# RWKV-7 attention with a SoLU block on one core: two products turned over, one head's features as weights

## The chip, the core and the metric

The kernel runs on one core of one Trainium2 chip. The metric is the device time of one execution in microseconds (us); three executions of the kernel before took 1791.39, 1779.59 and 1787.28, median 1787.28. All arithmetic is float32. TensorE (PE) executes one float32 product as two instruction pairs, each a weight load (PEld in the profile) and a stream of the other operand, so counts in the trace are twice the counts of products in the program.

## The reference: what is computed

Four batches, eight heads, 768 tokens, 40 features a head. Each head keeps a 40 x 40 state that every token reads, decays and updates; the outputs of the eight heads are laid side by side (320 features) and go through a dense layer of 1024, a softmax-weighted activation, a normalisation and a dense layer back to 320.

```python
for t in range(S):
    y[:, :, t] = np.einsum('bhd,bhde->bhe', rt, state)
    Sa = np.einsum('bhde,bhe->bhd', state, at)
    state_decay = state * wt[:, :, None, :] - np.einsum('bhd,bhe->bhde', Sa, bt)
    state = state_decay + np.einsum('bhd,bhe->bhde', vt, kt)
...
x = np.ascontiguousarray(attn_out.transpose(0, 2, 1, 3)).reshape(B * S, H * D)
h = x @ w_in
e = np.exp(h - h_max)
sm = e / (np.sum(e, axis=-1, keepdims=True) + 1e-09)
solu = h * sm
ln = (solu - mu) / np.sqrt(var + 1e-06) * g_ln
return (ln @ w_out).astype(np.float32)
```

## The kernel before

The tokens are cut into 24 chunks of 128 tokens of one batch. Within a chunk the recurrence is a triangular system (I + N) U = X0, one 128 x 128 system per head, so a chunk is a chain of matrix products. The main loop takes chunk i through its second half while chunk i + 1 goes through its first half; `in_turn` emits the pieces of two parts by turns, a `yield` ending a piece.

- `decay` takes the logs of the decays and, by products with 0/1 matrices, sums them along the chunk: `pcum`. Line 247 gives the factors of the keys, line 250 (320 columns) those of `a` and of the output, and line 252 (four products with 4 columns each) the factors that carry the state to mid-chunk and to the end.
- `attend` transposes `a`, `b`, `k`, `v` and `r` (`transposed`, line 199, copied out by ScalarE at line 201) and forms 128 x 128 score matrices per head (`scores`, line 209, masked by VectorE at line 211): `nt` (the matrix N), `psi`, `lamv`. Their products contract over 64 rows; the even heads lie in rows 0 to 63 and the odd heads in rows 64 to 127.
- `solve` inverts I + N of the next chunk by doubling: five levels of `py` (line 315), `pz` (line 325) and a transposition `pt` (line 299), each with two halves p that VectorE and ScalarE serve in between, and one last level (lines 340 and 347). It is most of TensorE's work and is what the other parts are interleaved with.
- `recurrence`: `px` (lines 363 and 366) gives X0 (tile `x0`); `pu` (line 373) multiplies it by the inverse: the 128 x 128 inverse of a head is the weights and 40 columns of X0 stream. ScalarE negates it into `nu` (128 tokens x features). The state update `pst` (line 381) uses `nu`; `nu` is transposed into `nuT` for the scores `lamu`.
- `finish` is `readout` and `mlp`. In `readout`, `pyo` collects r times the state (line 408) and, for each head, `lamv` and `lamu` as 128 x 128 weights with 40 columns of the keys streaming (line 413). VectorE scales the result (line 417, tile `x`), three transpositions `pxT` (line 421) and a ScalarE copy (line 423) make `xT`, the weights of `h` (line 433). `mlp` then runs the activation on VectorE and ScalarE, transposes the result (`plnT`, line 465) and multiplies by the second matrix (`po`, line 470).

The order of instructions on each engine is set by a scheduler at build time that emits what its own model finds ready by priority; at run time each engine follows that order and waits on semaphores. Loads and stores are issued by the SP queue in its order.

Of the kernel before, what the change touches and what calls it, by code (L numbers as in the profile page):

```python
# [56 lines left out]
def kernel(  # L57
# [25 lines left out]
    NK = -(-DM // P)  # L83
# [34 lines left out]
    lw_t = zeroed("lw", [P, H, 64], 2)  # L118
    ah_t = zeroed("ah", [P, H, 64], 2)
# [5 lines left out]
    x_t = zeroed("x", [P, NK * P], 2)  # L125
    y_lev = zeroed("ylev", [P, 2, G, P], len(LEVELS))
    y_last = const.tile([P, 2, G, 64], FP32, name="y_last")
    w_in = zeroed("w_in", [P, NK, DFF], 1)[0]
# [44 lines left out]
    def weights():  # L173
        nc.scalar.dma_start(out=g_rows, in_=moe_g_ln.rearrange("(c p) -> c p", p=P))
        for kt in range(NK):
            n = min(P, DM - kt * P)
            load_weight(w_in[0:n, kt, :], moe_w_in[kt * P:kt * P + n, :])
# [17 lines left out]
    def transposed(name, src, tag="T", bufs=4):  # L195
        """[128 tokens, 8 x 64] -> [(head of the pair, feature), pair, 128 tokens]"""
# [4 lines left out]
        nc.scalar.copy(out=o.rearrange("p g t -> p (g t)"), in_=t)  # L201
        return o

    def scores(name, lhs, rhs, dst):
        """dst[s, head, t] = lhs_s . rhs_t where s < t, else 0"""
# [18 lines left out]
    def load(i):  # L224
# [7 lines left out]
        for n, ap in (("w", w), ("k", k), ("b", b), ("a", a)):  # L232
            d["raw_" + n] = raw.tile([P, H, D], FP32, tag="raw_" + n, name="raw_" + n)
            nc.sync.dma_start(out=d["raw_" + n], in_=src(ap))
        nc.sync.dma_start(out=rv[:, 1, :, 0:D], in_=src(v))
        nc.sync.dma_start(out=rv[:, 0, :, 0:D], in_=src(r))

    def decay(i):
        """The decayed keys of chunk i, their growth and decay counted from mid-chunk."""
        d = st[i]  # L240
        lw, kb, ah = lw_t[i % 2], kb_t[i % 3], ah_t[i % 2]
        d["kb"] = kb
        nc.scalar.activation(out=lw[:, :, 0:D], in_=d["raw_w"], func=AF.Ln)
        ex = d["ex"] = two.tile([P, DM + 16], FP32, tag="ex", name="ex", bufs=4)
# [4 lines left out]
        t = bank("pcum")  # L249
        nc.tensor.matmul(t[:, 0:DM], lhsT=c_("cum_ex"), rhs=lw[:, :, 0:D], start=True, stop=True)  # L250
        for g in range(G):
            nc.tensor.matmul(t[:, DM + 4 * g:DM + 4 * g + 4], lhsT=pair(lw, g), rhs=c_("half"),
                             start=True, stop=True)
        nc.scalar.activation(out=ex, in_=t[:, 0:DM + 16], func=AF.Exp)
        for j, n in enumerate("kb"):
            nc.gpsimd.tensor_tensor(out=kb[:, j, :, 0:D], in0=d["raw_" + n], in1=heads(inv), op=ALU.mult)
        nc.gpsimd.tensor_tensor(out=ah[:, :, 0:D], in0=d["raw_a"], in1=heads(ex[:, 0:DM]), op=ALU.mult)
        f = ex[:, DM:].rearrange("p (g f c) -> p g f c", g=G, f=2)
# [4 lines left out]
        d["ah"] = ah  # L263

    def attend(i):
        """What chunk i needs of itself alone: its tokens' products with each other."""
        d = st[i]
        kb = d["kb"]
        aT = d["aT"] = transposed("aT", d["ah"], "aT", 2)
# [65 lines left out]
        # the last doubling is one block of 64 x 64, and T itself is not needed any more  # L335
# [17 lines left out]
    def recurrence(i):  # L353
# [14 lines left out]
        x0 = two.tile([P, DM], FP32, tag="x0", name="x0")  # L368
        nc.scalar.copy(out=x0, in_=t[:, 0:DM])
        yield  # L370
        t = bank("pu")
        for h in range(H):
            nc.tensor.matmul(t[:, h * D:h * D + D], lhsT=d["tinvT"][:, h % 2, h // 2, :],  # L373
                             rhs=x0[:, h * D:h * D + D], start=True, stop=True)
        nc.scalar.mul(out=nu[:, :, 0:D], in_=heads(t[:, 0:DM]), mul=-1.0)
# [16 lines left out]
        nuT = transposed("nuT", nu)  # L392
        lamu = d["lamu"] = wide("lamu", 1)
        scores("lamu", nuT, d["rT"], lamu)
# [6 lines left out]
    def readout(i):  # L401
# [4 lines left out]
        if ci:  # L406
            for g in range(G):
                nc.tensor.matmul(t[:, g * 80:g * 80 + 80], lhsT=d["rT"][:, g, :],
                                 rhs=d["sT"][:, g, :].rearrange("p (c d) -> p c d", c=2)[:, :, 0:D],
                                 start=g == 0, stop=False, skip_group_check=True)  # L410
        for h in range(H):
            for j, lam in enumerate((d["lamv"], d["lamu"])):
                nc.tensor.matmul(t[:, h * D:h * D + D], lhsT=lam[:, h % 2, h // 2, :], rhs=kb[:, j, h, 0:D],  # L413
                                 start=not ci and h == 0 and j == 0, stop=j == 1, skip_group_check=True)
        yield
        x = x_t[i % 2]
        nc.vector.tensor_tensor(out=x[:, 0:DM], in0=t[:, 0:DM], in1=d["ex"][:, 0:DM], op=ALU.mult)
# [25 lines left out]
        # (q / c - mean) / sqrt(var / c^2 + eps) = (q - mean_q) / sqrt(var_q + eps c^2), c = esum + 1e-9  # L443
# [86 lines left out]
```

## Time and profile before

| | |
|---|---|
| three executions | 1791.39, 1779.59, 1787.28 us (median 1787.28) |
| profiled execution, span of its instructions | 1769.0 us |
| PE busy, PEld busy | 91%, 80% of the span |
| DVE, ACT, POOL busy | 32%, 23%, 14% |
| mean granted TensorE clock | 0.898 of full speed |
| chain that ended last: PE, DVE, issue, ACT | 80%, 10%, 5%, 4% |

The profile gives the span, from the first to the last instruction; the lowest of the three executions is 10.6 us and the median 18.3 us above it. PE is the matrix stream, PEld the weight load that runs beside it, DVE is VectorE, ACT is ScalarE, POOL is GpSimd and SP issues transfers. A line Lnn is the line of the kernel printed above. The granted clock has two levels, 2.4 GHz (1.0) and 1.2 GHz (0.5); a stretch that shows 0.72 was partly at each.

### The profile page before, as it was taken

Reading aid. Unit: us, or ns where it says so; the run is one execution under the profiler, and the core shown is the slowest. Engines: PE = TensorE matmul, PEld = TensorE weight load, DVE = VectorE, ACT = ScalarE, POOL = GpSimd, SP = SyncE. Lnnn points to the kernel's source line nnn. Section 1 sums busy time; section 2 is a strip of 40 time slices with the busy share of each in tenths; the row PEclk is TensorE's granted clock in tenths of the full one; section 3 lists DMA queues with packets and bytes.
Section 4 is the critical chain, followed back from the end, with each engine's and each line's share of the span. In section 5 each row is a group of like instructions: output and inputs, shape, how many; then the busy total and the mean of one; then the engine's idle time right before and its main releaser. Section 6 shows DMA issues by size and latency. Waiting matters only on the chain.

```text
span 1769.0 us, 26279 instructions
## 1 busy us (share of the span) xinstructions
PE 1607.7 (91%) x11353; PEld 1407.5 (80%) x11353; DVE 570.5 (32%) x1306; ACT 399.5 (23%) x765; POOL 242.6 (14%) x274
## 2 busy tenths in 40 slices
PE   3999999899999999999989989999999999998997
PEld 2888787787877878879778778788787887877875
DVE  7783222322232222222232332223222322222231
ACT  1122122221221222222222222122122222222221
POOL 6131010210110101101021021011010110102100
PEclk9689898998998988988999999899898998898996
DMA  7220110100101101011011010010110100000000
GB/s 133 54 60 8 20 27 4 23 12 19 24 5 23 27 5 23 12 20 23 5 23 27 4 23 16 16 23 5 23 27 4 19 12 16 5 4 1 5 4 4
DMA packets 157267, 34.95 MB, mean 20 GB/s; under 512 B 150616, under 2 KB 154720, under 8 KB 157152
## 3 DMA queue, kind: packets, MB, share of 16 engines
q1 hardware_dynamic: 153216, 27.54, 8.6%
q10 hardware_dynamic: 3936, 5.75, 1.1%
q8 instruction: 89, 1.46, 0.3%
q14 instruction: 26, 0.21, 0.0%
HBM read 29.34 MB, written 3.93 MB: 19 GB/s over the span
## 4 chain that ended last, share of the span: by engine, by line
PE 80%; DVE 10%; issue 5%; ACT 4%; DMA 1%; POOL 1%; POOLq 0%; ACTq 0%
PE py L315 15%; PE pz L325 13%; PE po L470 7%; PE h L433 7%; PE pt L299 6%; PE pyo L413 5%; PE pu L373 2%; PE plamv L209 2%; PE px L366 2%; PE plamu L209 2%; DVE tinvT L328 2%; PE pst L381 2%; PE plnT L465 2%; PE ppsi L209 2%; PE pnt L209 2%
## 5 line engine op out<-in xcount | busy, mean ns | idle before, releaser
L315 PEld LDWEIGHTS py<-tinv,nt 128*128 128x128 f32 x1920 | 283.6, 233 | 24.0 <-ACT tinv L300 13.0
L315 PE MATMUL py<-tinv,nt 128*128 128x64 f32 x1920 | 292.4, 317 | 0.7 <-ACT tinv L300 0.5
L325 PE MATMUL pz<-tinvT,ylev 128*128 128x64 f32 x1920 | 271.1, 301 | 0.9 <-DVE ylev L317 0.9
L325 PEld LDWEIGHTS pz<-tinvT,ylev 128*128 128x128 f32 x1920 | 262.8, 218 | 5.9 <-DVE ylev L317 1.0
L300 ACT COPY tinv<-pt 128x512 f32<-128x512 f32 x288 | 165.8, 587 | 328.8 <-PE pt L299 302.6
L299 PE MATMUL pt<-cst,tinvT 128*128 128x128 f32 x1152 | 189.4, 300 | 21.7 <-DVE tinvT L328 16.8
L317 DVE TENSOR_TENSOR ylev<-py,cst 128x256 f32<-128x256 f32 x240 | 101.6, 423 | 258.6 <-PE py L315 258.6
L299 PEld LDWEIGHTS pt<-cst,tinvT 128*128 128x128 f32 x1152 | 147.6, 160 | 45.1 <-DVE tinvT L328 44.0
L328 DVE TENSOR_TENSOR tinvT<-tinvT,pz 128x256 f32<-128x256 f32 x240 | 100.7, 419 | 255.3 <-PE pz L325 255.2
L303 POOL TENSOR_TENSOR tinvT<-nt,cst 128x512 f32<-128x512 f32 x48 | 61.3, 1277 | 732.6 <-DVE nt L211 732.6
L470 PE MATMUL po<-w,lnT 128*128 128x320 f32 x384 | 134.7, 514 | 0.0
L433 PE MATMUL h<-w_in,xT 128*128 128x512 f32 x288 | 133.1, 612 | 0.6 <-ACT xT L423 0.6
L470 PEld LDWEIGHTS po<-w,lnT 128*128 128x128 f32 x384 | 87.4, 235 | 37.3 <-issue 17.4
L433 PEld LDWEIGHTS h<-w_in,xT 128*128 128x128 f32 x288 | 56.3, 204 | 60.7 <-issue 59.6
L465 PE MATMUL plnT<-cst,e 128*128 128x128 f32 x192 | 37.1, 357 | 65.7 <-DVE e L457 65.7
L455 POOL TENSOR_TENSOR rs<-c,mhalf 128x1 f32<-128x1 f32 x24 | 13.2, 550 | 565.1 <-DVE c L454 565.1
L465 PEld LDWEIGHTS plnT<-cst,e 128*128 128x128 f32 x192 | 28.7, 178 | 71.3 <-issue 71.3
L437 DVE TENSOR_REDUCE nmax<-h 128x1 f32<-128x1024 f32 x24 | 29.4, 1225 | 159.4 <-PE h L433 159.4
L413 PE MATMUL pyo<-kb,lamu 128*128 128x40 f32 x384 | 80.4, 296 | 0.0
L413 PE MATMUL pyo<-kb,lamv 128*128 128x40 f32 x384 | 78.7, 292 | 0.0
L423 ACT COPY xT<-pxT 128x384 f32<-128x384 f32 x24 | 11.5, 479 | 238.7 <-PE pxT L421 234.1
L211 DVE TENSOR_TENSOR nt<-pnt,cst 128x512 f32<-128x512 f32 x48 | 31.1, 686 | 104.8 <-PE pnt L209 104.8
(118 smaller groups left out, 2020.7 us busy)
## 6 DMA issues: line engine op xcount, KB each, us to landing
raw_w<-in_w_dram SPq DMA_DIRECT2D x24, 160.0 KB, 3.5
raw_k<-in_k_dram SPq DMA_DIRECT2D x24, 160.0 KB, 2.5
raw_b<-in_b_dram SPq DMA_DIRECT2D x24, 160.0 KB, 3.1
raw_a<-in_a_dram SPq DMA_DIRECT2D x24, 160.0 KB, 3.2
rv<-in_v_dram SPq DMA_DIRECT2D x24, 160.0 KB, 2.7
rv<-in_r_dram SPq DMA_DIRECT2D x24, 160.0 KB, 2.7
out_dram<-osb SPq DMA_DIRECT2D x24, 160.0 KB, 1.8
bits<-in_moe_w_in_dram ACTq DMA_DIRECT2D x8, 256.0 KB, 3.7
```

The costliest lines, as they stand in the source:

```text
L209: nc.tensor.matmul(t[:, g * P:(g + 1) * P], lhsT=lhs[rows(p), g, :], rhs=rhs[rows(p), g, :], start=True, stop=True)
L299: nc.tensor.transpose(out=t[:, g * P:(g + 1) * P], in_=tinvT[:, p, g, :], identity=ident)
L300: nc.scalar.copy(out=tinv[:, p].rearrange("q g c -> q (g c)"), in_=t)
L303: nc.gpsimd.tensor_tensor(out=tinvT[:, p], in0=nt[:, p], in1=pairm.unsqueeze(1).to_broadcast([P, G, P]), op=ALU.mult)
L315: nc.tensor.matmul(t[:, g * 64:g * 64 + 64], lhsT=nt[:, p, g, :], rhs=cols(tinv[:, p, g, :], m, 0), start=True, stop=True)
L317: nc.vector.tensor_tensor(out=cols(y[:, p], m, 0), in0=t[:, 0:256].rearrange("q (g k m) -> q g k m", g=G, m=m), in1=lev[:, li].rearrange(" ...
L325: nc.tensor.matmul(t[:, g * 64:g * 64 + 64], lhsT=y[:, p, g, :], rhs=cols(tinvT[:, p, g, :], m, 1), start=True, stop=True)
L328: nc.vector.tensor_tensor(out=view, in0=view, in1=t[:, 0:256].rearrange("q (g k m) -> q g k m", g=G, m=m), op=ALU.subtract)
L413: nc.tensor.matmul(t[:, h * D:h * D + D], lhsT=lam[:, h % 2, h // 2, :], rhs=kb[:, j, h, 0:D], start=not ci and h == 0 and j == 0, stop=j ...
L433: nc.tensor.matmul(h[:, hh], lhsT=d["xT"][:, kt, :], rhs=w_in[:, kt, hh], start=kt == 0, stop=kt == NK - 1)
L465: nc.tensor.transpose(out=t[:, j * P:(j + 1) * P], in_=ln[:, f * P:(f + 1) * P], identity=ident)
L470: nc.tensor.matmul(o[:, 0:DM], lhsT=lnT[:, f, :], rhs=w2[:, f, :], start=f == 0, stop=f == NF - 1)
```

## The change

`pu` and the per-head part of `pyo` are turned over. Where a 128 x 128 matrix (the inverse, `lamv`, `lamu`) was the weights and 40 columns streamed, now a head's 64 columns (40 features and 24 zeros) are the weights and the 128 columns of the matrix stream. The result of an even head goes to partitions 0 to 63 and of an odd head to 64 to 127, which are two column halves of the array. So U arrives transposed (`nuT`), is transposed back into `nu` for the state update, and the scores `lamu` need only `nuT`. The output factors are computed transposed (`exT`, `pcx`), so `a` is transposed raw and scaled by VectorE on its way out. y leaves VectorE already transposed, with each head in its own 64-row slot; eight transfers of 40 x 128 numbers pack it into `xT` (three groups of 120, 120 and 80 rows). The three transpositions `pxT` and their copy are gone, and three more empty pieces stand ahead of `mlp`. Comments are dropped too.

```diff
-    NK = -(-DM // P)
+    NK, KT = 3, 120
...
-    def transposed(name, src, tag="T", bufs=4):
+    def transposed(name, src, tag="T", bufs=3, scale=None):
...
-        nc.scalar.copy(out=o.rearrange("p g t -> p (g t)"), in_=t)
+        if scale is None:
+            nc.scalar.copy(out=o.rearrange("p g t -> p (g t)"), in_=t)
+        else:
+            nc.vector.tensor_tensor(out=o, in0=t.rearrange("p (g t) -> p g t", g=G), in1=scale, op=ALU.mult)
...
-        t = bank("pcum")
-        nc.tensor.matmul(t[:, 0:DM], lhsT=c_("cum_ex"), rhs=lw[:, :, 0:D], start=True, stop=True)
-        for g in range(G):
-            nc.tensor.matmul(t[:, DM + 4 * g:DM + 4 * g + 4], lhsT=pair(lw, g), rhs=c_("half"),
-                             start=True, stop=True)
-        nc.scalar.activation(out=ex, in_=t[:, 0:DM + 16], func=AF.Exp)
+        lo = where["cum_ex"][0]
+        for j in range(2):
+            t = bank("pcx")
+            for g in range(2):
+                nc.tensor.matmul(t[:, g * 132:g * 132 + 132], lhsT=pair(lw, 2 * j + g), rhs=cst[:, lo:lo + 132],
+                                 start=True, stop=True)
+            nc.scalar.activation(out=exT[:, 2 * j:2 * j + 2].rearrange("p g t -> p (g t)"), in_=t[:, 0:264], func=AF.Exp)
...
-        aT = d["aT"] = transposed("aT", d["ah"], "aT", 2)
+        aT = d["aT"] = transposed("aT", d["a"], "aT", 2, d["exT"][:, :, 0:P])
...
         for h in range(H):
-            nc.tensor.matmul(t[:, h * D:h * D + D], lhsT=d["tinvT"][:, h % 2, h // 2, :],
-                             rhs=x0[:, h * D:h * D + D], start=True, stop=True)
-        nc.scalar.mul(out=nu[:, :, 0:D], in_=heads(t[:, 0:DM]), mul=-1.0)
+            nc.tensor.matmul(t[rows(h % 2), h // 2 * P:h // 2 * P + P], lhsT=x0[:, h, :],
+                             rhs=d["tinvT"][:, h % 2, h // 2, :], start=True, stop=True)
+        nuT = two.tile([P, G, P], FP32, tag="nuT", name="nuT", bufs=1)
+        nc.scalar.mul(out=nuT.rearrange("p g t -> p (g t)"), in_=t, mul=-1.0)
+        yield
+        t = bank("pnu")
+        for g in range(G):
+            nc.tensor.transpose(out=t[:, g * P:(g + 1) * P], in_=nuT[:, g, :], identity=ident)
+        nc.scalar.copy(out=nu.rearrange("p h c -> p (h c)"), in_=t)
+        lamu = d["lamu"] = wide("lamu", 1)
+        scores("lamu", nuT, d["rT"], lamu)
...
-        nuT = transposed("nuT", nu)
-        lamu = d["lamu"] = wide("lamu", 1)
-        scores("lamu", nuT, d["rT"], lamu)
...
-                nc.tensor.matmul(t[:, g * 80:g * 80 + 80], lhsT=d["rT"][:, g, :],
-                                 rhs=d["sT"][:, g, :].rearrange("p (c d) -> p c d", c=2)[:, :, 0:D],
+                nc.tensor.matmul(t[:, g * P:g * P + P], lhsT=d["sT"][:, g, :], rhs=d["rT"][:, g, :],
                                  start=g == 0, stop=False, skip_group_check=True)
         for h in range(H):
             for j, lam in enumerate((d["lamv"], d["lamu"])):
-                nc.tensor.matmul(t[:, h * D:h * D + D], lhsT=lam[:, h % 2, h // 2, :], rhs=kb[:, j, h, 0:D],
-                                 start=not ci and h == 0 and j == 0, stop=j == 1, skip_group_check=True)
-        yield
-        x = x_t[i % 2]
-        nc.vector.tensor_tensor(out=x[:, 0:DM], in0=t[:, 0:DM], in1=d["ex"][:, 0:DM], op=ALU.mult)
-        yield
-        t = bank("pxT")
-        for kt in range(NK):
-            nc.tensor.transpose(out=t[:, kt * P:(kt + 1) * P], in_=x[:, kt * P:(kt + 1) * P], identity=ident)
-        d["xT"] = two.tile([P, NK, P], FP32, tag="xT", name="xT")
-        nc.scalar.copy(out=d["xT"].rearrange("p k t -> p (k t)"), in_=t[:, 0:NK * P])
-        yield
+                nc.tensor.matmul(t[rows(h % 2), h // 2 * P:h // 2 * P + P], lhsT=kb[:, j, h, :],
+                                 rhs=lam[:, h % 2, h // 2, :], start=not ci and h < 2 and j == 0, stop=j == 1,
+                                 skip_group_check=True)
+        yield
+        x = two.tile([P, G, P], FP32, tag="x", name="x")
+        nc.vector.tensor_tensor(out=x, in0=t.rearrange("p (g t) -> p g t", g=G), in1=d["exT"][:, :, 0:P], op=ALU.mult)
+        xT = d["xT"] = two.tile([P, NK, P], FP32, tag="xT", name="xT")
+        for h in range(H):
+            nc.sync.dma_start(out=xT[h % 3 * D:h % 3 * D + D, h // 3, :], in_=x[64 * (h % 2):64 * (h % 2) + D, h // 2, :])
+        for _ in range(4):
+            yield
```

How the instructions move. In the rows below each product stands once (`x8` means eight products of that form in a row); `pu`, `pyo` and the like are the accumulators, with the weights and the stream behind the arrow.

TensorE, the recurrence of a middle chunk, from `pu` to the scores `lamu`, before:

```order
L373 MATMUL pu<-x_6123,tinvT 128x40 x8
L199 MATMUL pvT<-cst,rv_92 128x128 x4
L199 MATMUL prT<-cst,rv_92 128x128 x4
L209 MATMUL plamv<-rT,vT 128x128 x8
L381 MATMUL pst<-rv_96,kb_90 128x80
L381 MATMUL pst<-nu_100,kb_90 128x80
...
L199 MATMUL psT<-cst,sm_112 128x128 x4
L199 MATMUL pnuT<-cst,nu_100 128x128 x4
L209 MATMUL plamu<-rT,nuT 128x128 x8
```

The same stretch after the change:

```order
L377 MATMUL pu<-tinvT,x_118 64x128 x8
L199 MATMUL pvT<-cst,rv_94 128x128 x4
L199 MATMUL prT<-cst,rv_94 128x128 x4
L212 MATMUL plamv<-rT,vT 128x128 x8
L384 MATMUL pnu<-cst,nuT 128x128 x4
L212 MATMUL plamu<-rT,nuT 128x128 x8
L393 MATMUL pst<-rv_98,kb_92 128x80
L393 MATMUL pst<-nu_102,kb_92 128x80
...
L199 MATMUL psT<-cst,sm_114 128x128 x4
```

The scores `lamu` stood right behind the transposition whose ScalarE copy they need; now the tile they need, `nuT`, is copied out while `pvT`, `prT` and `plamv` run, and it is the state update that needs the copy of `pnu`, with `plamu` in between.

TensorE, from the read-out to the dense layer, before:

```order
L408 MATMUL pyo<-sT,rT 128x80 x4
L413 MATMUL pyo<-kb_90,lamv 128x40
L413 MATMUL pyo<-kb_90,lamu 128x40
...
L315 MATMUL py<-tinv,nt 128x64 x8
L325 MATMUL pz<-tinvT,ylev_118 128x64 x8
L421 MATMUL pxT<-cst,x_116 128x128 x3
L299 MATMUL pt<-cst,tinvT 128x128 x8
```

After the change:

```order
L417 MATMUL pyo<-rT,sT 128x128 x4
L421 MATMUL pyo<-lamv,kb_92 64x128
L421 MATMUL pyo<-lamu,kb_92 64x128
...
L319 MATMUL py<-tinv,nt 128x64 x8
L329 MATMUL pz<-tinvT,ylev_120 128x64 x8
L303 MATMUL pt<-cst,tinvT 128x128 x8
L319 MATMUL py<-tinv,nt 128x64 x8
L441 MATMUL h<-w_in,xT 128x512
L329 MATMUL pz<-tinvT,ylev_122 128x64 x8
L441 MATMUL h<-w_in,xT 128x512 x5
```

`h` stood behind the first level of `solve`; now the first product of `h` stands behind the next level's `py`, and the other five behind its `pz`.

The SP queue after the change, from one chunk's store to the next:

```order
L482 DMA out_dram<-osb 128x320
L239 DMA a_84<-in_a_dram 128x8x40
L241 DMA rv_96<-in_r_dram 128x8x40
L240 DMA rv_94<-in_v_dram 128x8x40
L237 DMA raw_k<-in_k_dram 128x8x40
L237 DMA raw_b<-in_b_dram 128x8x40
L237 DMA raw_w<-in_w_dram 128x8x40
L429 DMA xT<-x 40x128 x8
```

The eight packing transfers stand behind the six loads of a later chunk and ahead of the store; before, SP had only the loads and the store.

## Rows read from the trace of the kernel before

**Rows 1.** Page, the chain that ended last, shares of the span by engine

```profile
PE 80%; DVE 10%; issue 5%; ACT 4%; DMA 1%; POOL 1%; POOLq 0%; ACTq 0%
```

**Rows 2.** Timeline of PE, a read-out at full clock: start, us, engine, line, operation, xcount

```profile
896.43 0.70 PE L250 MATMUL pcum<-lw,cst 128*128 128x320 f32 x2
896.96 0.95 PE L252 MATMUL pcum<-cst,lw 128*128 128x4 f32 x8
897.77 1.07 PE L299 MATMUL pt<-cst,tinvT 128*128 128x128 f32 x8
898.68 1.02 PE L408 MATMUL pyo<-sT,rT 128*128 128x80 f32 x8
899.53 0.35 PE L413 MATMUL pyo<-kb,lamv 128*128 128x40 f32 x2
...
903.07 1.98 PE L315 MATMUL py<-tinv,nt 128*128 128x64 f32 x16
906.67 0.50 PE L421 MATMUL pxT<-cst,x 128*128 128x128 f32 x3
907.00 1.07 PE L299 MATMUL pt<-cst,tinvT 128*128 128x128 f32 x8
907.91 3.60 PE L433 MATMUL h<-w_in,xT 128*128 128x512 f32 x8
```

**Rows 3.** Timeline of PE, scores of two row halves, then the product of U

```profile
811.89 0.27 PE L209 MATMUL ppsi<-aT,kT 64*128 64x128 f32 x1
811.89 0.27 PE L209 MATMUL pnt<-aT,bT 64*128 64x128 f32 x1
...
813.31 1.98 PE L373 MATMUL pu<-x,tinvT 128*128 128x40 f32 x16
815.12 0.64 PE L199 MATMUL pvT<-cst,rv 128*128 128x128 f32 x4
...
816.92 0.37 PE L209 MATMUL plamv<-rT,vT 64*128 64x128 f32 x1 [0.73 <-ACT rT L201]
```

**Rows 4.** Timeline of PE, the last level of solve: weights 64 wide

```profile
804.04 1.34 PE L340 MATMUL py<-tinv,nt 64*64 64x64 f32 x15
805.17 0.27 PE L347 MATMUL pz<-tinvT,y_last 64*64 64x64 f32 x1
```

**Rows 5.** Windows: stretch, length, busy time of five engines, granted clock, DMA share, GB/s

```profile
185.10:203.60 18.50, 18.50 (x91) 15.35 (x90) 2.19 (x5) 2.65 (x6) 1.15 (x3) 0.72 0.21 36
1605.30:1623.80 18.50, 18.50 (x91) 15.55 (x90) 2.19 (x5) 1.65 (x3) 1.00 (x3) 0.72 0.00 1
327.30:344.20 16.90, 16.90 (x91) 14.03 (x90) 2.19 (x5) 2.72 (x6) 1.89 (x4) 0.80 0.23 39
1463.80:1480.70 16.90, 16.90 (x91) 14.03 (x90) 2.19 (x5) 1.80 (x4) 1.26 (x3) 0.80 0.17 30
899.50:913.20 13.70, 13.70 (x91) 10.78 (x91) 2.19 (x5) 1.78 (x4) 1.05 (x3) 1.00 0.27 46
211.60:222.10 10.50, 10.50 (x43) 8.53 (x43) 0.85 (x2) 1.09 (x2) 0.00 (x0) 0.67 0.01 2
```

**Rows 6.** Waits: engine and line, what it waited for, us in all, times, longest

```profile
PE plnT L465 <- DVE e L457: 65.7, 24, 7.1
PE plamu L209 <- ACT nuT L201: 17.7, 24, 1.1
```

**Rows 7.** Page, transfers (KB each, us from issue to landing) and a group

```profile
raw_w<-in_w_dram SPq DMA_DIRECT2D x24, 160.0 KB, 3.5
out_dram<-osb SPq DMA_DIRECT2D x24, 160.0 KB, 1.8
L211 DVE TENSOR_TENSOR nt<-pnt,cst 128x512 f32<-128x512 f32 x48 | 31.1, 686 | 104.8 <-PE pnt L209 104.8
```

**Rows 8.** Timeline of the SP queue: two loads issued one after the other

```profile
827.76 0.37 SPq L234 DMA_DIRECT2D raw_a<-in_a_dram  x1
828.22 0.87 SPq L234 DMA_DIRECT2D raw_w<-in_w_dram  x1
```

More of the change, by code (lines that the diff above doesn't have):

```diff
@@ L118 @@
     lw_t = zeroed("lw", [P, H, 64], 2)
-    ah_t = zeroed("ah", [P, H, 64], 2)
+    a_t = zeroed("a", [P, H, 64], 3)
     kb_t = zeroed("kb", [P, 2, H, 64], 3)
@@ L124 @@
     sm_t = zeroed("sm", [P, G, 2, 64], 2)
-    x_t = zeroed("x", [P, NK * P], 2)
+    x0_t = zeroed("x0", [P, H, 64], 2)
     y_lev = zeroed("ylev", [P, 2, G, P], len(LEVELS))
     y_last = const.tile([P, 2, G, 64], FP32, name="y_last")
-    w_in = zeroed("w_in", [P, NK, DFF], 1)[0]
+    w_in = const.tile([P, NK, DFF], FP32, name="w_in")
     w2 = const.tile([P, NF, DM], FP32, name="w2")
@@ L175, in weights @@
         for kt in range(NK):
-            n = min(P, DM - kt * P)
-            load_weight(w_in[0:n, kt, :], moe_w_in[kt * P:kt * P + n, :])
+            n = min(KT, DM - kt * KT)
+            load_weight(w_in[0:n, kt, :], moe_w_in[kt * KT:kt * KT + n, :])
         pg = bank("pg")
@@ L231, in load @@
         rv = d["rv"] = rv_t[i % 3]
-        for n, ap in (("w", w), ("k", k), ("b", b), ("a", a)):
+        for n, ap in (("w", w), ("k", k), ("b", b)):
             d["raw_" + n] = raw.tile([P, H, D], FP32, tag="raw_" + n, name="raw_" + n)
             nc.sync.dma_start(out=d["raw_" + n], in_=src(ap))
+        d["a"] = a_t[i % 3]
+        nc.sync.dma_start(out=d["a"][:, :, 0:D], in_=src(a))
         nc.sync.dma_start(out=rv[:, 1, :, 0:D], in_=src(v))
@@ L240, in decay @@
         d = st[i]
-        lw, kb, ah = lw_t[i % 2], kb_t[i % 3], ah_t[i % 2]
+        lw, kb = lw_t[i % 2], kb_t[i % 3]
         d["kb"] = kb
         nc.scalar.activation(out=lw[:, :, 0:D], in_=d["raw_w"], func=AF.Ln)
-        ex = d["ex"] = two.tile([P, DM + 16], FP32, tag="ex", name="ex", bufs=4)
+        exT = d["exT"] = two.tile([P, G, P + 4], FP32, tag="exT", name="exT", bufs=3)
         inv = two.tile([P, DM], FP32, tag="inv", name="inv")
@@ L248, in decay @@
         nc.scalar.activation(out=inv, in_=t[:, 0:DM], func=AF.Exp)
-        t = bank("pcum")
-        nc.tensor.matmul(t[:, 0:DM], lhsT=c_("cum_ex"), rhs=lw[:, :, 0:D], start=True, stop=True)
-        for g in range(G):
-            nc.tensor.matmul(t[:, DM + 4 * g:DM + 4 * g + 4], lhsT=pair(lw, g), rhs=c_("half"),
-                             start=True, stop=True)
-        nc.scalar.activation(out=ex, in_=t[:, 0:DM + 16], func=AF.Exp)
+        lo = where["cum_ex"][0]
[5 more added lines that the diff above has]
+            nc.scalar.activation(out=exT[:, 2 * j:2 * j + 2].rearrange("p g t -> p (g t)"), in_=t[:, 0:264], func=AF.Exp)
         for j, n in enumerate("kb"):
             nc.gpsimd.tensor_tensor(out=kb[:, j, :, 0:D], in0=d["raw_" + n], in1=heads(inv), op=ALU.mult)
-        nc.gpsimd.tensor_tensor(out=ah[:, :, 0:D], in0=d["raw_a"], in1=heads(ex[:, 0:DM]), op=ALU.mult)
-        f = ex[:, DM:].rearrange("p (g f c) -> p g f c", g=G, f=2)
+        f = exT[:, :, P:].rearrange("p g (f c) -> p g f c", f=2)
         d["to_mid"] = f[:, :, 1, :]
@@ L262, in decay @@
                                 in1=c_("diag").rearrange("p (g c) -> p g c", c=2), op=ALU.mult)
-        d["ah"] = ah
     def attend(i):
@@ L367, in recurrence @@
                              start=not ci and h == 0, stop=True, skip_group_check=True)
-        x0 = two.tile([P, DM], FP32, tag="x0", name="x0")
-        nc.scalar.copy(out=x0, in_=t[:, 0:DM])
+        x0 = x0_t[i % 2]
+        nc.scalar.copy(out=x0[:, :, 0:D], in_=heads(t[:, 0:DM]))
         yield
@@ L432, in mlp @@
             for kt in range(NK):
-                nc.tensor.matmul(h[:, hh], lhsT=d["xT"][:, kt, :], rhs=w_in[:, kt, hh],
+                n = min(KT, DM - kt * KT)
+                nc.tensor.matmul(h[:, hh], lhsT=d["xT"][0:n, kt, :], rhs=w_in[0:n, kt, hh],
                                  start=kt == 0, stop=kt == NK - 1)
```

## The prediction

> **What bounds the kernel now.** I read four views in this order. The chain of waits first: 80% of the span is PE work, and no other engine holds more than 10% [rows 1]; so only what shortens PE's own time, a wait of PE or its clock counts. Then PE's timeline of one chunk at full clock, for the price of each kind of product (the distance from the start of one row to the start of the next, over its instructions). A pair of 128 wide weights and 40 columns costs 3.54 us / 32 = 0.111 us in the read-out [rows 2] and 1.81 / 16 = 0.113 in `pu` [rows 3]; with 4 columns 0.81 / 8 = 0.101, with 80 columns 0.85 / 8 = 0.106, with 320 columns 0.53 / 2 = 0.265 [rows 2]. So up to 80 columns a pair costs its 128 wide load, and a long stream costs 0.265 / 320 x 128 = 0.106 us per 128 columns. 128 columns streaming are thus as dear as 128 columns of weights, and turning a product over saves nothing by itself: it takes a price of about 0.11 per pair from the load and puts it on the stream. What can be gained is that two column halves work at once.
>
> Third, the granted clock by stretches. From the first read-out product to the end of `h` a chunk takes 13.7 us at clock 1.00, but in 18 chunks the clock is at its lower level for part of it: nine of about 18.5 us at 0.72 (first and last shown) and nine of about 16.9 at 0.80 (first and last shown) [rows 5]. That is 9 x 18.5 x 0.28 + 9 x 16.9 x 0.20 = 77 us of lost speed. What PE does just before each fall is the stretch of rows 2: four products with 4 columns, eight transpositions, then 80 and 40 columns. Fourth, the waits: PE waits 65.7 us in all for the activation before `plnT`, behind which the clock falls again (10.5 us at 0.67) [rows 5, 6], and 17.7 us for `nuT` [rows 6].
>
> **The change part by part, per chunk at full clock.**
>
> `pu` and the 32 head pairs of `pyo` keep their 48 instructions. Whether two column halves run side by side no row shows. The nearest: scores of two row halves start at the same 811.89 where one half follows the other [rows 3], so the array does take two partial products at once, when they use other rows. Bounds for a pair: 0.056 (half of 0.111) and 0.111 (one after the other); a pair with 64 wide weights and 64 columns costs (805.17 - 804.04) / 15 = 0.075 [rows 4]. I take 0.065, between side by side and that row, since heads alternate halves every two instructions in `pu` and every four in `pyo`. `pu` 1.81 to 1.04, `pyo` 3.54 to 2.08: -2.23 us, over 24 chunks **-53** (bounds -64 and 0).
>
> A rule speaks on each side. The Trainium skill, "TensorEngine Tiling (Array Packing)", section Performance Considerations, recommends just this swap with two column tiles for a narrow stream, at up to twice the speed; by it alone the pair would cost 0.056 and this term would be -64. The row halves of rows 3 agree in kind, no row shows column halves.
>
> The sums of the decays: lines 250 and 252 take 1.34 us [rows 2]; four products of 132 columns are 8 pairs at 132 x 0.265 / 320 = 0.109, 0.88. -0.46, **-11**. The state part of `pyo` streams 128 columns for 80: 0.106 stays 0.106. `pxT`, 0.33 [rows 2]: **-8**. The wait for `nuT` before `plamu` goes, because `nuT` is copied while `pvT`, `prT` and `plamv` run: **-18** [rows 6]. What is late next there is `rT`: its wait of 0.73 [rows 3] grows, since ScalarE copies 512 columns of `nuT` before `vT` where it copied 320; by an estimate 0.15, **+4**. The state update's new wait for the copy of `pnu` is covered by `plamu` (16 instructions, about 1.7 us). Scaling `aT` on VectorE takes 0.69 [rows 7] for ScalarE's copy: nothing, VectorE is on 10% of the chain.
>
> The packing. After the last `pyo`, VectorE scales `x` (0.69, [rows 7]), SP issues eight transfers 0.46 apart [rows 8], and each lands 1.8 to 3.5 us after its issue [rows 7], both bounds from transfers eight times as large. The first three, which the first product of `h` needs, are there after 0.7 + 2 x 0.46 + 1.8 to 3.5 = 3.4 to 5.1 us, all eight after 5.7 to 7.4. PE meanwhile has `py`, `pz` (3.60 together), `pt` (0.91) and the next `py` (1.80): it reaches `h` after 6.3 us, and the rest of `h` after that first product (0.85) and another `pz` (1.80), at 9.0 [rows 2]. Hidden, with about 1.2 us to spare; beyond that each microsecond costs 23. On SP the store waits behind the transfers, as it would for its own data; the loads behind it run more than a chunk ahead. In the last chunk nothing covers: 5.7 us in place of about 1.3 for `x`, `pxT` and the copy, **+5**. Three more changes of tile shape a chunk, an estimate of at most one pair (0.11) each: **+8**.
>
> The clock. All narrow products ahead of the fall but the transpositions are replaced by streams of 128 or 132 columns. The bounds: none of the 77 us comes back, or all. Five of the other six chunks had no fall with the old products (one of them in rows 5), so the stretch is close to holding its clock even now; I take all: **-77**. The wait before `plnT` keeps its work on both sides (`py`, `pz`, `pt` in another order), so its falls stay.
>
> Sum: 1769 - 53 - 11 - 8 - 18 + 4 + 5 + 8 - 77 = 1619 us of span. The median of the three executions lies 18.3 us above the profiled span (the lowest 10.6), and I add that: **1637 us** against 1787.28.
>
> **The rivals.**
>
> *The halves take turns.* Both halves use all 128 rows, and rows 3 show overlap for separate rows alone. Then a pair stays at 0.111: 1637 + 53 = 1690. Against it: the outputs and the weights do lie apart.
>
> *The clock still falls.* The stretch still holds eight transpositions, and two levels of `solve` (64 columns to a 128 wide load) instead of one follow before `h` streams 512 columns. Against it: the rest of `solve` is the same work. 1637 + 77 = 1714; with the first rival 1767.
>
> *The packing is late.* If each of the eight transfers started only when the one before had landed, `xT` would be whole after 0.7 + 8 x 1.8 = 15.1 us, 6.1 behind the slot at 9.0: 23 x 6.1 = 140, 1777. Against: loads are issued 0.46 apart without such a wait [rows 8].
>
> *Load and stream lie bare, slower than before.* If a load into one half can't go on while the other half streams, a pair costs half of 0.101 plus 0.106 = 0.157 us, and 48 of them 7.5 for 5.35 us now; with the clock falling as before the time is 1637 + 77 + 24 x 48 x (0.157 - 0.065) = 1820. The turning point, with the falls kept, is a pair of 0.065 + (1787 - 1714) / 1152 = 0.128 us. Against: with full width weights the load does hide, 80 columns cost no more than 40 [rows 2]. The Trainium skill, "TensorE: Matmul & The Clock Gate", section Part 3: Packing small matmuls, says that a load overlaps a running product only where the row group differs, which here it never does; by that rule this is the outcome. The trace disagrees within one tile: 0.106 a pair at 80 columns has no room for a bare load. No row has it for column tiles.
>
> **How the numbers follow.** Forecast 0.62 (own range 1600 to 1665); halves in turn 0.16; clock still falls 0.11, both 0.03; packing late 0.04; bare loads 0.04. Below 1600 I see little: it takes 0.056 a pair and falls gone at `plnT` too. From 1600 to 1715 lie the first three cases, 0.89 together, some of which stray out; that is the range for 8 in 10. About 1% is what a measurement of this kernel can tell from no change. Faster by over 1% (under 1769): the first three, and half of the fourth, 0.90. Within 1%: the rest of that and most of the late packing, 0.05. Slower: 0.05.
>
> **What would show it.** Right: two `pyo` instructions of different halves starting at the same time and about 2.1 us from the first to `py`; clock 1.00 from `pcum` to `h`; no wait of `plamu`; `h` following `py` without a wait; the wait of `plnT` as before. Wrong: `pyo` at 3.5 us or more, a clock of 0.5 in the two levels of `solve` before `h`, PE idle for a transfer at `h`, or a longer wait at `plnT`, into which the saved time would fall if the activation, not PE, set that stretch.

## The result and the profile after

The changed kernel took 1625.82 us (median; 1625.54 to 1627.05 in four runs), the kernel before 1789.34 us on the same chip (1779.59 to 1799.23, four runs). The ratio is 0.910, 95% interval 0.904 to 0.916: 9% faster. The forecast was 1637, its range 1600 to 1715. The profiled execution of the changed kernel has a span of 1625.3 us and took 1627.05; before, the span was 1769.0.

The page of the changed kernel: its span, and the chain that ended last, which answers to [rows 1].

```profile
span 1625.3 us, 26345 instructions
PE 77%; DVE 11%; issue 5%; ACT 5%; DMA 1%; POOL 1%; ACTq 0%; POOLq 0%; DVEq 0%
```

PE still holds the chain, with 77% where it had 80%, of a span that is 8% shorter. PE's timeline of one chunk of the changed kernel follows, from the sums of the decays to the layer norm's transpositions (start, us, engine, line, operation, count, and in brackets idle time before it); it answers to [rows 2].

```profile
828.07 1.06 PE L258 MATMUL pcx<-cst,lw 128*128 128x132 f32 x8
828.97 1.04 PE L303 MATMUL pt<-cst,tinvT 128*128 128x128 f32 x8
829.84 1.06 PE L417 MATMUL pyo<-rT,sT 128*128 128x128 f32 x8
830.83 0.45 PE L421 MATMUL pyo<-lamv,kb 128*64 128x128 f32 x4
...
832.41 0.44 PE L421 MATMUL pyo<-lamu,kb 128*64 128x128 f32 x4
832.78 2.00 PE L319 MATMUL py<-tinv,nt 128*128 128x64 f32 x16
...
839.57 1.08 PE L441 MATMUL h<-w_in,xT 120*128 120x512 f32 x2
840.49 1.90 PE L329 MATMUL pz<-tinvT,ylev 128*128 128x64 f32 x16
842.22 4.52 PE L441 MATMUL h<-w_in,xT 120*128 120x512 f32 x10
846.58 1.04 PE L303 MATMUL pt<-cst,tinvT 128*128 128x128 f32 x8
847.91 2.00 PE L319 MATMUL py<-tinv,nt 128*128 128x64 f32 x16 [0.29 <-ACT tinv L304]
...
855.41 1.94 PE L473 MATMUL plnT<-cst,e 128*128 128x128 f32 x8 [3.72 <-DVE e L465]
```

The 32 head pairs of `pyo` go from 830.83 to 832.78: 1.95 us, 0.061 a pair, where they took 3.54 [rows 2]. Each row of `pyo` holds four instructions, two heads of two halves, in 0.22 us from row to row; a row of before held two in the same time. `h` starts without an idle time in front of it, and the one long wait is that of `plnT`, 3.72 us.

The same timeline later, at the product of U; it answers to [rows 3].

```profile
883.38 1.09 PE L377 MATMUL pu<-tinvT,x 128*64 128x128 f32 x16
884.41 0.66 PE L199 MATMUL pvT<-cst,rv 128*128 128x128 f32 x4
...
886.23 1.71 PE L212 MATMUL plamv<-rT,vT 64*128 64x128 f32 x16 [0.73 <-ACT rT L202]
887.87 0.66 PE L384 MATMUL pnu<-cst,nuT 128*128 128x128 f32 x4
888.45 1.71 PE L212 MATMUL plamu<-rT,nuT 64*128 64x128 f32 x16
```

`pu` takes 1.03 us for 1.81, `plamu` follows without a wait, and the wait for `rT` is the 0.73 of before.

The granted clock by stretches of the changed kernel (columns as in [rows 5]): the read-out to `h` in two chunks, then the stretch behind `plnT`.

```profile
828.00:842.20 14.20, 14.06 (x131) 12.81 (x130) 3.97 (x9) 3.99 (x9) 2.54 (x4) 1.00 0.32 59
1475.40:1489.60 14.20, 14.05 (x112) 11.32 (x107) 4.08 (x9) 1.17 (x2) 0.12 (x1) 1.00 0.04 12
855.40:864.30 8.90, 8.89 (x33) 7.16 (x34) 0.00 (x0) 2.34 (x4) 0.00 (x0) 0.68 0.01 2
```

In these two chunks, as in all from the second to the last but one, the clock does not fall behind the read-out; behind `plnT` it falls as before (0.67 there in [rows 5]).

PE's waits in the changed kernel, which answer to [rows 6].

```profile
PE plnT L473 <- DVE e L465: 92.7, 24, 7.1
PE plamv L212 <- ACT rT L202: 17.4, 24, 0.7
PE py L319 <- ACT tinv L304: 7.0, 24, 0.3
PE h L441 <- DMA xT<-x: 4.5, 2, 4.3
PE pt L303 <- DVE tinvT L332: 4.2, 24, 0.5
```

The wait for `nuT` is gone, that of `plnT` has grown from 65.7 to 92.7 us, and the transfers of the packing cost 4.5 us in the whole kernel, 4.3 of them in the last chunk. The SP queue beside the timeline above, which answers to [rows 8]:

```profile
831.02 0.91 SPq L237 DMA_DIRECT2D raw_w<-in_w_dram  x1
833.61 6.03 SPq L429 DMA_DIRECT2D xT<-x  x8
```

Eight transfers hold SP for 6.03 us, about 0.75 each, and the last is issued at 839.64, 2.6 us before `h` needs it at 842.22.

### The profile page after: what moved, and what is told of

Its sections match the earlier page's. It is cut to its first block, busy times and chain, and to the rows that moved or that the text cites. A ratio compares the mean times of both kernels' runs of the same rounds, so it can differ in the third digit from the quotient of the medians.

```text
span 1625.3 us, 26345 instructions
## 1 busy us (share of the span) xinstructions
PE 1449.2 (89%) x11233; PEld 1251.3 (77%) x11233; DVE 586.9 (36%) x1330; ACT 383.5 (24%) x741; POOL 220.8 (14%) x250
## 4 chain that ended last, share of the span: by engine, by line
PE 77%; DVE 11%; issue 5%; ACT 5%; DMA 1%; POOL 1%; ACTq 0%; POOLq 0%; DVEq 0%
PE py L319 14%; PE pz L329 11%; PE h L441 7%; PE pt L303 7%; PE po L478 7%; DVE tinvT L332 3%; PE plnT L473 3%; PE pyo L421 3%; PE px L370 3%; PE plamv L212 3%; PE pst L393 2%; PE plamu L212 2%; PE ppsi L212 2%; PE pnt L212 2%; DVE e L450 2%
## 5 line engine op out<-in xcount | busy, mean ns | idle before, releaser
L319 PEld LDWEIGHTS py<-tinv,nt 128*128 128x128 f32 x1920 | 232.0, 196 | 29.8 <-ACT tinv L304 21.5
L319 PE MATMUL py<-tinv,nt 128*128 128x64 f32 x1920 | 243.9, 281 | 7.0 <-ACT tinv L304 7.0
L329 PEld LDWEIGHTS pz<-tinvT,ylev 128*128 128x128 f32 x1920 | 235.0, 198 | 14.5 <-issue 11.0
L329 PE MATMUL pz<-tinvT,ylev 128*128 128x64 f32 x1920 | 242.3, 281 | 3.0 <-DVE ylev L321 2.9
L441 PE MATMUL h<-w_in,xT 120*128 120x512 f32 (+1 forms) x288 | 139.3, 620 | 4.5 <-DMA xT<-x 4.5
L473 PE MATMUL plnT<-cst,e 128*128 128x128 f32 x192 | 46.2, 422 | 92.7 <-DVE e L465 92.7
L441 PEld LDWEIGHTS h<-w_in,xT 120*128 120x128 f32 (+1 forms) x288 | 52.5, 196 | 53.9 <-issue 52.8
L474 ACT COPY lnT<-plnT 128x512 f32<-128x512 f32 x48 | 28.1, 585 | 174.9 <-PE plnT L473 174.9
L309 POOL TENSOR_TENSOR tinvT<-tinvT,cst 128x512 f32<-128x512 f32 x48 | 61.2, 1275 | 3.8
L212 PE MATMUL pnt<-aT,bT 64*128 64x128 f32 x384 | 43.8, 297 | 17.6 <-ACT bT L202 17.6
```

Of the source, the lines that this page charges most:

```text
L212: nc.tensor.matmul(t[:, g * P:(g + 1) * P], lhsT=lhs[rows(p), g, :], rhs=rhs[rows(p), g, :], start=True, stop=True)
L309: nc.gpsimd.tensor_tensor(out=tinvT[:, p], in0=tinvT[:, p], in1=ident.unsqueeze(1).to_broadcast([P, G, P]), op=ALU.add)
L319: nc.tensor.matmul(t[:, g * 64:g * 64 + 64], lhsT=nt[:, p, g, :], rhs=cols(tinv[:, p, g, :], m, 0), start=True, stop=True)
L329: nc.tensor.matmul(t[:, g * 64:g * 64 + 64], lhsT=y[:, p, g, :], rhs=cols(tinvT[:, p, g, :], m, 1), start=True, stop=True)
L441: nc.tensor.matmul(h[:, hh], lhsT=d["xT"][0:n, kt, :], rhs=w_in[0:n, kt, hh], start=kt == 0, stop=kt == NK - 1)
L473: nc.tensor.transpose(out=t[:, j * P:(j + 1) * P], in_=ln[:, f * P:(f + 1) * P], identity=ident)
```

## The experiments

**Do the two halves work side by side?** The changed kernel with the heads of one half behind one another:

```diff
-        for h in range(H):                      # in pu and in pyo
+        for h in (0, 2, 4, 6, 1, 3, 5, 7):
```

> The changed kernel with the heads of pu and of the read-out taken in the order 0, 2, 4, 6, 1, 3, 5, 7, so that the two column halves follow each other once and don't alternate; same instructions, same prices of load and stream. Theory: the gain of the two products comes from two halves working at once, so most pairs now cost 0.107 to 0.111 us in place of 0.061 and 0.064. 48 pairs a chunk less a few that still overlap at the one seam: about 45 x 0.047 x 24 = +51 us, 1677 (1660 to 1690), clock falls as in the changed kernel. Rival: the pair is cheap because its weights are 64 wide, whatever its neighbour; then 1626.

Measured: 1660.65 us, ratio to before 0.934 [0.927, 0.941], 35 us more than the changed kernel, at the low end of the forecast's range and far from the rival's 1626. PE's timeline of the read-out in this kernel:

```profile
911.51 0.43 PE L421 MATMUL pyo<-lamv,kb 128*64 128x128 f32 x2
911.78 0.38 PE L421 MATMUL pyo<-lamu,kb 128*64 128x128 f32 x2
...
912.88 0.44 PE L421 MATMUL pyo<-lamv,kb 128*64 128x128 f32 x4
913.10 0.44 PE L421 MATMUL pyo<-lamu,kb 128*64 128x128 f32 x4
913.37 0.38 PE L421 MATMUL pyo<-lamv,kb 128*64 128x128 f32 x2
...
914.77 2.00 PE L319 MATMUL py<-tinv,nt 128*128 128x64 f32 x16
```

and of `pu`:

```profile
898.73 1.58 PE L377 MATMUL pu<-tinvT,x 128*64 128x128 f32 x16
900.25 0.66 PE L199 MATMUL pvT<-cst,rv 128*128 128x128 f32 x4
```

With the same instructions in another order a pair costs (914.77 - 911.51) / 32 = 0.102 us instead of 0.061. A step of 0.22 us holds two instructions of one half, except in the middle, where the last head of one half and the first of the other share a step and four fit. So the two halves run at once here only if their instructions stand next to each other, and then they do. `pu` has (900.25 - 898.73) / 16 = 0.095 a pair for 0.064. By these prices the pairs of both cost 24 x (16 x 0.031 + 32 x 0.041) = 43 us more; 35 were measured, and the spans differ by 32 (1657.3 for 1625.3). The changed kernel's own time, here and below, is that of its four runs in the section on the result; the median of the kernel before moves between 1775 and 1789 us from experiment to experiment, so a difference of a few us between two of them says nothing.

**What drops the clock behind the read-out?** The kernel before with the read-out's products at 64 columns a head and 128 in the state part, both widened together (VectorE, which scales the result, leaves the added columns out):

```diff
-    matmul(t[:, g * 80:g * 80 + 80], lhsT=d["rT"][:, g, :], rhs=d["sT"][:, g, :]...[:, :, 0:D], ...)
+    matmul(t[:, g * P:g * P + P], lhsT=d["rT"][:, g, :], rhs=d["sT"][:, g, :], ...)
-    matmul(t[:, h * D:h * D + D], lhsT=lam[:, h % 2, h // 2, :], rhs=kb[:, j, h, 0:D], ...)
+    matmul(t[:, h * 64:h * 64 + 64], lhsT=lam[:, h % 2, h // 2, :], rhs=kb[:, j, h, :], ...)
```

> The kernel before, with the read-out streaming the 64 columns of a head with its zeros in place of its 40 (and 128 for 80 in the state part); one 128 wide load per pair as before, so at full clock the pairs cost the same 0.107 to 0.111. Theory: the clock fell behind the read-out because the products there stream few columns; with 64 the falls there go, and with them up to 77 us of the profiled execution: about 1700 to 1715, clock 1.00 from the read-out to h. Rival: the four products with 4 columns and the eight transpositions ahead of it, or the loads, decide; then the falls stay and the time is that of the kernel before, 1780 to 1800.

and, as the other suspect, the four products of 4 columns alone at 128 columns (the exponentials behind them are then two ScalarE instructions instead of one):

```diff
-    matmul(t[:, DM + 4 * g:DM + 4 * g + 4], lhsT=pair(lw, g), rhs=c_("half"), ...)
+    matmul(u[:, g * P:g * P + P], lhsT=pair(lw, g), rhs=cst[:, hi - P:hi], ...)
```

> The kernel before, with the four products that stream 4 columns streaming 128 (the other 124 columns of the result are not used), and the exponentials taken in two ScalarE instructions in place of one; the read-out is as before. Pairs at full clock cost 0.107 for 0.101: +1 us over the run, and about 0.2 us a chunk on ScalarE, covered. If the 0.8 us of 4 columns tips the clock, the falls behind the read-out go: about 1705 to 1720. If the 40 columns of the read-out do, nothing changes: 1780 to 1800. If both count, some chunks fall and some do not: in between.

Measured: 1732.94 us for the first, ratio 0.973 [0.964, 0.982]; 1773.95 for the second, ratio 1.000 [0.996, 1.003]. The start of the kernel before, and of the first kernel, with one read-out to `h` of the latter:

```profile
0.00:130.00 130.00, 95.68 (x571) 87.40 (x572) 103.22 (x341) 23.29 (x44) 47.66 (x57) 0.83 0.41 84
0.00:130.00 130.00, 96.61 (x493) 89.84 (x494) 97.11 (x310) 21.63 (x41) 46.17 (x56) 0.69 0.37 79
884.80:898.50 13.70, 13.70 (x92) 10.78 (x90) 2.20 (x6) 1.69 (x4) 0.97 (x3) 1.00 0.26 45
```

A read-out to `h` of the second kernel:

```profile
903.20:921.70 18.50, 18.50 (x86) 15.76 (x86) 2.18 (x5) 1.66 (x4) 1.01 (x3) 0.63 0.20 34
```

With 64 columns the clock begins to fall behind the read-out in no chunk; with the 4-column products widened it still does in 19 chunks, as it did in 18 before. PE is busy all the time in both windows (13.70 of 13.70, 18.50 of 18.50). It was behind the read-out's products of 40 and 80 columns, then, and not for idle time or the 4 columns, that the clock fell there. The gain is 32 to 64 us by the interval, not 77: the start of this kernel runs at 0.69 over 130 us where the kernel before had 0.83, which alone is 130 x 0.14 = 18 us, and the falls behind `plnT` add up to 177 us at the lower clock where the kernel before has 136, another 20 us lost.

**Is the packing hidden, and by what?** The changed kernel with one step of `solve` between the packing and `h` instead of four, and the changed kernel with each transfer cut in two:

```diff
-        for _ in range(4):
-            yield
+        yield
```

> The changed kernel without the three empty pieces ahead of the dense layer, so that h stands earlier among the pieces of solve and PE comes to it sooner. Theory: the packing takes about 3.4 us to the first three transfers and 5.7 to all eight after the last read-out product, which the pieces cover; without them PE waits at h for the transfers, 1 to 3 us a chunk, and the clock may fall there too: 1650 to 1720. Rival: the transfers are quick enough for any place, or the scheduler leaves h where it is: 1620 to 1635.

```diff
-    nc.sync.dma_start(out=xT[..., h // 3, :], in_=x[..., h // 2, :])
+    for q in (slice(0, 64), slice(64, 128)):
+        nc.sync.dma_start(out=xT[..., h // 3, q], in_=x[..., h // 2, q])
```

> The changed kernel with each of the eight transfers of the packing cut into two of 64 tokens: 16 transfers of half the bytes. Theory (a transfer costs SP 0.7 us whatever its size, so that the eight are only just hidden): issue takes 16 x 0.76 = 12 us in place of 6, the rest of h waits 4 to 6 us a chunk for its last transfers: 23 x 4 to 6 = 92 to 138 us, 1715 to 1765. Rival (the cost goes by bytes, 0.35 us each): the packing ends where it did, 1626 to 1635.

Measured: 1680.10 us, ratio 0.945 [0.938, 0.952], and 1710.36, ratio 0.959 [0.956, 0.962]; 54 and 85 us over the changed kernel. The first lies in its range and the second 5 us under its own, but for a reason that was not theirs. PE's waits in the first

```profile
PE plnT L472 <- DVE e L464: 150.7, 24, 7.1
PE h L440 <- DMA xT<-x: 5.0, 4, 4.3
```

and in the second

```profile
PE plnT L474 <- DVE e L466: 169.9, 24, 7.1
PE h L442 <- DMA xT<-x: 11.2, 5, 6.9
```

show `h` waiting 5 and 11 us for the transfers in all. What grew is the wait of `plnT`, by 58 and 77 us. In the first program `h` stands within half a piece of `solve` of where it stood, late enough for the transfers, and it is `plnT` that comes three pieces sooner; in the second `plnT` stands where it did and `h` further back, with its last part right ahead of `plnT`. In both, less is left behind `h` to cover the layer norm, as the timeline of the first shows:

```profile
864.27 3.66 PE L440 MATMUL h<-w_in,xT 80*128 80x512 f32 x8
867.77 1.00 PE L329 MATMUL pz<-tinvT,ylev 128*128 128x64 f32 x8
875.06 1.94 PE L472 MATMUL plnT<-cst,e 128*128 128x128 f32 x8 [6.29 <-DVE e L464]
```

Half a `pz` stands between `h` and `plnT` where the changed kernel has `pt`, `py` and `pz`. What a transfer that PE really waited for would cost in each chunk was not measured. SP's issue of the sixteen halves

```profile
801.35 12.04 SPq L430 DMA_DIRECT2D xT<-x  x16
```

takes 12.04 us for 6.03, so a transfer costs SP the same 0.75 us at half the bytes.

**What is `pu` worth alone?** The kernel before with `pu` turned over and `nuT` taken straight from it, the read-out as it was:

```diff
+            matmul(t[rows(h % 2), h // 2 * P:h // 2 * P + P], lhsT=x0[:, h, :],
+                   rhs=d["tinvT"][:, h % 2, h // 2, :], ...)
+        nc.scalar.mul(out=nuT.rearrange("p g t -> p (g t)"), in_=t, mul=-1.0)
...
+            nc.tensor.transpose(out=t[:, g * P:(g + 1) * P], in_=nuT[:, g, :], identity=ident)
-        nuT = transposed("nuT", nu)
```

> The kernel before with pu alone turned over (features as weights, 128 tokens moving, two heads in two column halves; nuT copied straight from it and nu made from nuT), the read-out as before. Theory: 24 x (1.81 - 1.03) = 19 us of products and the 17.7 us of the wait for nuT come back, the pair of transpositions stays; the clock falls behind the read-out stay, at 17 to 19 chunks: 36 us less than before, 1735 to 1765 (the falls of the kernel before vary its time by some 15 us either way). Rival (the turned products alone keep the clock up): as above and half of 154 us more, about 1680.

Measured: 1758.43 us, ratio 0.986 [0.982, 0.991], 29 us less than before (16 to 33 by the interval); 36 were expected. The window of a read-out to `h` and beyond in this kernel:

```profile
890.00:910.00 20.00, 20.00 (x105) 17.13 (x103) 2.85 (x6) 2.58 (x5) 1.76 (x4) 0.74 0.20 34
```

The clock still falls there, in 20 chunks: the turned `pu` does not keep it up, the turned read-out does. The mean clock of this execution, the longest of the four, is 0.875 for 0.898, so that its span of 1767.6 us is that of the kernel before (1769.0): falls took back what the products and the wait for `nuT` gave.

**What is left: the wait of `plnT`.** The changed kernel with `plnT` two and three steps of `solve` later:

```diff
         yield
         yield
+        yield
+        yield
+        yield                                   # the third in one of the two
         lnT = two.tile(...)
```

> The changed kernel with plnT two steps later (behind one more pt and py, 2.9 us of work). By the theory of the kernel with three steps the wait is gone or nearly so here too, except what VectorE's queue sets: 24 x 1.6 to 1.9 = 38 to 46 us of waits back, and of the clock what a shorter idle time leaves: 1520 to 1590, within 15 us of three steps. By the rival 1615 to 1630.

> The changed kernel with plnT put three steps of solve later (behind one more pt, py and pz), so that PE has 4.7 us of work where it waits 92.7 us in all (3.72 us in the chunk of 855.41) for the layer norm. Theory (the loss behind h is the wait, and the clock falls because PE stands idle before plnT): the wait falls to some 1.5 to 2 us a chunk, because solve's own subtractions stand in VectorE's queue between the layer norm's operations until 853.5, so 24 x about 2 = 45 to 50 us come back; and up to half of the 140 us at the lower clock behind it, 70. Time 1510 to 1580. Rival (VectorE, not the place of plnT, sets the stretch): the wait goes from plnT to pt, py or pz at the same length, PE idles there, the clock falls there: 1615 to 1630.

Measured: 1545.65 us, ratio 0.866 [0.863, 0.869], and 1546.51, ratio 0.866 [0.862, 0.870], 80 us under the changed kernel in both, within 1 us of one another and within both forecasts: the wait did not move elsewhere at the same length. PE's waits with three steps:

```profile
PE pt L303 <- DVE tinvT L332: 31.3, 70, 0.9
PE plnT L476 <- DVE e L465: 7.1, 1, 7.1
```

The wait of `plnT` is left in the last chunk alone, and 31 us stand at `pt`, for the subtractions of `solve` behind the layer norm's statistics in VectorE's queue. Falls remain in six chunks just behind that `pt`: its second half in one of them, and the window from 813.1 to 823.3 behind it:

```profile
812.22 1.12 PE L303 MATMUL pt<-cst,tinvT 128*128 128x128 f32 x4 [0.93 <-DVE tinvT L332]
813.10:823.30 10.20, 10.20 (x52) 10.04 (x51) 2.50 (x5) 2.48 (x5) 0.00 (x1) 0.55 0.00 0
```

So the statistics were put behind both subtractions (PE's order is that of the kernel with three steps):

```diff
+        yield
+        yield
         bs = small.tile(...)
...
         yield
         yield
+        yield
         lnT = two.tile(...)
```

> The kernel with plnT three steps later, and in VectorE's queue the layer norm's statistics behind both of solve's subtractions instead of between them; PE's order is the same. Theory (what is left of the wait, 31.3 us before pt, is VectorE's queue): the second pt no longer waits 0.93 us a chunk, 20 to 25 us come back, and with less idle time fewer falls of the clock behind it: 1505 to 1530. Rival (the wait goes to plnT, whose activation now ends about 1 us later, or nothing changes at the clock): 1535 to 1550.

Measured: 1493.39 us, ratio to before 0.842 [0.835, 0.848], better than expected, and the fastest version: 132 us under the changed kernel. The wait at `pt`, and the clock over 1323 us of this kernel:

```profile
PE pt L303 <- DVE tinvT L332: 8.5, 47, 0.5
```

```profile
138.00:1461.00 1323.00, 1272.63 (x10639) 1103.88 (x10637) 472.73 (x967) 349.24 (x692) 175.86 (x194) 1.00 0.10 21
```

Of the 53 us under the kernel with three steps the wait gives 23, as expected. For the rest there is the clock, full from 138 to 1461, that is in every chunk but the first and the last: the six falls that are gone were 10.2 us each at half speed, 31 us.

## Why the prediction was right, and where its terms were off

Against the span: 1769.0 - 1625.3 = 143.7 us came back, and 150 were summed.

**The products.** By rows of the same place, before and after, a chunk: `pyo` 3.54 to 1.95, `pu` 1.81 to 1.03, the sums of the decays 1.34 to 0.90, `pxT` 0.33 to nothing, the state part 0.85 to 0.99. That is 3.00 a chunk, 72 us in 24, against 53 + 11 + 8 less 8 for changes of tile shape, 64. The pair in two halves was put at 0.065 and is 0.061 in `pyo` and 0.064 in `pu`. Of the changes of tile shape, rows show the state part's 0.14 and, from the last row of `pyo` to `py`, 0.15 over the step of 0.22: 7 us in 24 chunks for these two, where 8 were put for three. The second is inside the 0.061; from row to row a pair is 0.22 / 4 = 0.055. The first experiment shows that the halves side by side are the cause. A full halving would be 0.056; the rows come within 0.005 of it. The turn is the one that the Trainium skill's "TensorEngine Tiling (Array Packing)", section Performance Considerations, recommends as "swap + 2× column tiling", and the trace agrees. The rule of the Trainium skill's "TensorE: Matmul & The Clock Gate", section Part 3: Packing small matmuls, that a load overlaps a running product only where the row group differs, doesn't hold here: all products of `pyo` use all rows, and a load left bare would make 0.157 a pair by the prediction's estimate.

**The clock.** The span and mean granted clock of the changed kernel's core:

```profile
core 0: 1625.3 us, clock 0.932
```

Before it was 0.898 over 1769.0 us. Taken as lost speed over the whole span, 1769.0 x 0.102 = 180 and 1625.3 x 0.068 = 111 us: 70 come back, and 77 were forecast. This counts the lower clock also where PE stands idle, as it now does longer before `plnT`, and there it costs nothing (the other three runs of the changed kernel have 0.921 or 0.922 and the same time); counted only while PE works, the traces have about 178 us lost before and 94 after, 84 back. All 18 falls behind the read-out are gone, the forecast's 77; the changed kernel has one in the first chunk, behind a wait of 1.23 us for `ylev`, and one in the last, behind 4.29 us for the transfers. The columns of the stream were named as the cause, and the experiments at 64 and at 4 columns bear that out for the 40- and 80-column products. The kernel at 64 columns would have been expected to give the 77 too, and gave 32 to 64: part went at its start and behind `plnT`, so a fall removed in one place isn't always a net gain of its length.

**The waits.** `nuT`: 17.7 gone, as forecast. `rT`: 17.4 for 17.9; the 4 us expected for ScalarE's longer copy ahead of it did not come. `plnT`: "keeps its work on both sides" was wrong, and a longer wait there, which the prediction named as a sign against it, came; its falls stayed, as forecast. The kernel before has there

```profile
PE pt L299 <- DVE tinvT L328: 16.8, 24, 0.8
...
913.06 1.89 PE L315 MATMUL py<-tinv,nt 128*128 128x64 f32 x16
...
921.21 1.06 PE L465 MATMUL plnT<-cst,e 128*128 128x128 f32 x8 [2.55 <-DVE e L457]
```

Before, `pt` stood between `pz` and `plnT` and had 16.8 us of waits of its own (the same subtractions in VectorE's queue); now it stands behind `plnT`, so that its wait became part of `plnT`'s. And the way from the end of `h` to `plnT` is longer (846.58 to 855.41, 8.83 us, for 8.15 before): `pt` comes first behind `h`, so its two copies stand ahead of the exponential on ScalarE, and both subtractions of `solve`, where it was one, among the layer norm's statistics on VectorE. Together, with `py`'s new wait for these copies, these waits went from 83 to 104 us: 21 lost that the sum did not have. It took less than the products and the clock gave, but it was the largest thing left to take, as the last experiments show.

**The packing.** Hidden, as forecast, but at closer quarters: SP takes 0.75 us for such a transfer, not the 0.46 read between two loads [rows 8]. SP is done 6.75 us after `x` starts to be scaled (832.89), where the forecast's numbers give 0.7 + 8 x 0.46 = 4.4; the slot it had counted on at 9.0 came at 9.3. The last chunk waits 4.3 us for the transfers where it waited 1.2 for `x` and the copy, 3 us more; 5 were forecast.

The parts, 72 + 18 + 84 less 21 and 3, are 150 against the 143.7; the 6 between them are in no row that I can name. That 150 were summed too is partly luck: the products and the clock gave 8 and 7 more than their terms, and the waits took 21 that no term held.

**The step from span to time.** The 18.3 us added to the span were the mis-sized step. In each of the runs here the time is the span and 1.7 to 1.9 us more (1627.05 and 1625.3 above). The profiled execution of before was one of its short ones: its runs lie between 1765.71 and 1804.16, at mean clocks from 0.910 down to 0.875. Of two runs of one experiment, spans 1767.1 and 1789.1, the mean clock is 0.898 and 0.885, which is 180 and 206 us lost, 26 for the 22 between them; a third of 1767.1 us has 0.910, so this is a tendency and no measure. The changed kernel, without the falls behind the read-out, varies by 1.5 us. Had 1.8 been added, the forecast would have been 1621, 5 below; two errors, the waits left out and this one, partly cancel, so that the forecast's 11 us from the result are luck in part.

Of the rivals, the halves taking turns is what the first experiment built, at 1661 (1690 was said of it, with a pair of 0.111 for the 0.102 it has). The clock still falling (but for the first and the last chunk), late packing and bare loads are excluded by the rows above.

## What to carry to other kernels

Where heads or groups stream fewer columns than the weights are wide, turn the product over and put two of them in two column halves in adjacent instructions: with the halves one after the other the same instructions came down from 0.111 us a pair to 0.102 only, in place of 0.061. Read PE's clock stretch by stretch before summing: what came back here by the clock was at least as much as by the products, and taking PE's remaining wait away, by moving one operation and reordering VectorE, was worth another 132 us, clock included. Of an instruction that is moved on PE, look where its wait goes, and take the way from span to run time from runs that show both.

## What was not expected of the hardware

- A transfer from SBUF to SBUF of 40 rows holds the SP queue 0.75 us, at 512 as at 256 bytes a row (6.03 us for eight, 12.04 for sixteen), where a load of 160 KB mostly holds it 0.37 (0.91 in the row above, over 2 at the longest).
- The kernel before lost its clock in the read-out with PE busy for all of the stretch; the same read-out widened from 40 to 64 columns and from 80 to 128, at the same 0.11 us a pair, kept it.
- In the fastest version the clock stayed at 2.4 GHz for 1323 us on end, with PE still waiting up to 0.73 us at a place in each chunk (for `rT`); in the kernel with three steps, with 0.93 us ahead of the second half of `pt`, it went to 1.2 GHz in six chunks.
